# Two fp16 pieces instead of two fp32r pieces in the products of an attention and MoE kernel

## The chip, the cores and the metric

The kernel runs on one core of a Trainium2 chip. The metric is the device time in microseconds, from the start to the end of one execution. The profile shows the engines TensorE (PE, with its weight loads as PEld), VectorE (DVE), ScalarE (ACT), GpSimd (POOL) and the DMA queues, of which SyncE (SP) issues nearly all.

## The reference

An attention with a decaying state runs over 768 tokens for 4 batches and 8 heads of width 48. Its output is the input of two dense products with a gate in between.

```python
for t in range(S):                                   # S = 768, D = 48
    cur = einsum('bhd,bhe->bhde', u[None] * kt, vt)
    y[:, :, t] = einsum('bhd,bhde->bhe', rt, state + cur)
    state = wt[:, :, :, None] * state + einsum('bhd,bhe->bhde', kt, vt)
x = y.transpose(0, 2, 1, 3).reshape(3072, 384)
h = x @ w_in                                         # 384 -> 2048
g = where(h >= 1, h, where(h <= -1, 0, (h + 1)**2 / 4))
out = g @ w_out                                      # 2048 -> 384, fp32
```

The weights come as float64. All other inputs and the output are fp32.

## The kernel before, in words

**Tiling.** The 3072 tokens are cut into 12 units of 256 for the attention and 6 blocks of 512 for the products. Unit u belongs to block u // 2. The 2048 hidden rows are cut into 16 slices `f` of 128. A *step* is one slice of one block: three input chunks of 128 rows are contracted into a bank `h` (line 1040), the gate is taken (lines 819 to 825), and the result is multiplied into the three output banks `acc` (line 1070), which gather over the 16 slices. `HALVES` cuts the first 8 slices of block 0 and the first 11 of block 1 into steps of 256 tokens, so that a block can start when only one of its units is there. There are 115 steps.

**Pieces.** All but the first 8 steps write each operand as a high and a low piece in fp32r, and add high x high, high x low and low x high: 9 matmuls in `product_in`, 9 in `product_out`. The first 8 steps multiply plain fp32 (`product_in_whole`, `product_out_whole`, lines 1046 and 1052), which the profile shows as two instructions per matmul.

**Gate of a step.** ACT computes relu(h/2 + 1/2) (line 819) and squares it (820), DVE takes max(min(g, 1), h) (821), ACT rounds it to `gh` (824), DVE subtracts for `gl` (825). Products of a step follow up to `LAG` = 2 steps later; there are two `h` banks and three sets of g, gh and gl.

**Weights.** `weight(f)` fetches a 768 KB tile of float64 bits (line 332), ACT and POOL take its words apart (342, 345, 346), DVE joins them to fp32 (336). `divide(f)` rounds to the high piece on ACT (358) and subtracts for the low piece on DVE (361). A fetch waits until ACT has read the raw tile of three fetches before. Raw tiles, fp32 tiles and pieces share one pool of 16 slots.

**Attention of a unit.** DVE makes decay products with scans (434, 429) and multiplies them in (455, 505). PE makes 64x64 products (475), state updates (533) and outputs (612). `yevac` takes the output to the pieces of x (ACT 699, DVE 697), and six small DMAs fill the rows that hold head remainders (747). For unit 0 the low piece is made on PE with a negative identity `minus` (709).

**Order.** Every operation is an entry of a plan with an engine, a cost and its dependences. `ORDER` is a written list of all entries. The program is emitted in that order, so it fixes the order on each engine's queue and on SP's. Near the end a check (`check`, then the PE dot of line 914 and a DVE compare) makes a flag; if it is set, the slower function `general` computes everything again.

Of the kernel before, what the change touches and what calls it, by code (L numbers as in the profile page):

```python
# [229 lines left out]
def attention_moe(tc, a):  # L230
    nc = tc.nc
    V, A, G, PE = nc.vector, nc.scalar, nc.gpsimd, nc.tensor
    plan = Plan()
# [907 lines left out]
```

## Time and profile before

| | us |
|---|---|
| median of 3 runs (lowest, highest) | 499.04 (498.68, 499.18) |
| span of the profiled execution | 495.2 |
| PE busy | 485.5 (98%) |
| DVE busy | 343.8 (69%) |
| ACT busy | 289.6 (58%) |
| POOL busy | 56.7 (11%) |

The span runs from the first to the last instruction of the profiled execution. No time of that one execution with what lies around its span is shown beside the three runs; the median is 3.8 us above the span. Busy shares are means over stages with different limits, so a change is judged from the stage in which it stands.

### The profile page before, as it was taken

The page shows a single profiled execution, that of the slowest core. Times are in us where ns is not written, and L with a number is a line of the kernel's source. Part 1 is how long each engine was busy: PE and PEld are TensorE (multiplying, and loading weights), DVE is VectorE, ACT ScalarE, POOL GpSimd, SP SyncE. Part 2 cuts the span into 40 slices and gives each one's busy share as a digit, 9 for nine tenths or more (in the row PEclk, how much of TensorE's full clock was granted, in tenths as well). Part 3 has the DMA queues.
Part 4 walks back from the last instruction along what each step waited for, and adds up shares of the span by engine and source line. Part 5 has one row for each costly group of instructions (what it writes and reads, how often), then busy time and mean ns, then how long its engine had stood idle before and what let it go on. Part 6 is the DMA issues. An engine that isn't in the chain of part 4 may idle for free.

```text
span 495.2 us, 12991 instructions
## 1 busy us (share of the span) xinstructions
PE 485.5 (98%) x5402; PEld 404.8 (82%) x5402; DVE 343.8 (69%) x597; ACT 289.6 (58%) x592; POOL 56.7 (11%) x60
## 2 busy tenths in 40 slices
PE   9799999999999999999999999999999999999997
PEld 4688998778999988888888888888888888888886
DVE  6899999998758768659679679469556745332333
ACT  3799889866656536746736646346626625552551
POOL 2332121300110101110110330020001000000000
PEclk9899999999999999999999999999999999999999
DMA  8995736225544344345245454225221110200001
GB/s 316 406 374 169 256 115 217 88 60 158 166 111 149 66 133 159 103 113 161 38 131 175 108 139 150 48 79 154 43 66 44 29 33 16 66 1 1 1 0 66
DMA packets 58749, 58.29 MB, mean 118 GB/s; under 512 B 38016, under 2 KB 47424, under 8 KB 58688
## 3 DMA queue, kind: packets, MB, share of 16 engines
q1 hardware_dynamic: 58256, 56.78, 37.4%
q8 instruction: 43, 0.70, 0.6%
q10 hardware_dynamic: 432, 0.66, 0.4%
q14 instruction: 18, 0.15, 0.1%
HBM read 46.34 MB, written 4.72 MB: 103 GB/s over the span
## 4 chain that ended last, share of the span: by engine, by line
PE 89%; DVE 5%; ACT 2%; issue 2%; DMA 1%; POOL 0%; DVEq 0%; SPq 0%; POOLq 0%
PE h L1040 37%; PE acc L1070 36%; PE bank L612 4%; PE bank L475 2%; PE bank L533 2%; PE acc L1052 2%; PE bank L1070 1%; PE h L1046 1%; PE bank L312 1%; DMA rk<-in_rk 1%; DVE r L481 1%; DVE wt L361 1%; PE acc L612 1%; DVE gl L825 1%; DVE rk L505 1%
## 5 line engine op out<-in xcount | busy, mean ns | idle before, releaser
L1040 PE MATMUL h<-x,wt 128*128 128x512 f32 (+1 forms) x963 | 207.4, 365 | 0.5 <-DVE g L821 0.4
L1040 PEld LDWEIGHTS h<-x,wt 128*128 128x128 f32 x963 | 162.5, 188 | 32.0 <-DVE g L821 0.9
L1070 PE MATMUL acc<-gh,wt 128*128 128x512 f32 (+1 forms) x642 | 146.4, 359 | 0.0
L821 DVE SCALAR_TENSOR_TENSOR g<-g,h 128x512 f32<-128x512 f32 (+1 forms) x115 | 67.8, 593 | 95.6 <-ACT g L820 95.1
L819 ACT ACTIVATE g<-h 128x512 f32<-128x512 f32 (+1 forms) x115 | 60.4, 526 | 119.2 <-PE h L1040 117.4
L1070 PEld LDWEIGHTS acc<-gh,wt 128*128 128x128 f32 x642 | 107.9, 188 | 18.7
L825 DVE TENSOR_TENSOR gl<-g,gh 128x512 fp32r<-128x512 f32 (+1 forms) x107 | 68.9, 648 | 17.1 <-ACT gh L824 10.6
L1070 PE MATMUL acc<-gl,wt 128*128 128x512 f32 (+1 forms) x321 | 80.7, 358 | 0.0
L824 ACT CAST gh<-g 128x512 fp32r<-128x512 f32 (+1 forms) x107 | 59.1, 556 | 33.1 <-DVE g L821 22.3
L820 ACT ACTIVATE g<-g 128x512 f32<-128x512 f32 (+1 forms) x115 | 64.4, 561 | 3.1
L1070 PEld LDWEIGHTS acc<-gl,wt 128*128 128x128 f32 x321 | 55.2, 188 | 9.1
L434 DVE TENSOR_TENSOR_SCAN p<-wq,seeds 128x514 f32<-128x514 f32 x24 | 30.8, 1283 | 10.8 <-DMA kt<-p 7.2
L501 POOL TENSOR_TENSOR r<-cst,d 128x512 f32<-128x512 f32 x16 | 17.0, 1084 | 152.2 <-DVE d L498 71.8
L429 DVE TENSOR_TENSOR_SCAN y<-wq,seeds 128x514 f32<-128x514 f32 x24 | 30.1, 1254 | 0.8
L346 POOL CAST rr<-fl 128x768 f16<-128x768 f32 x16 | 21.3, 1332 | 71.2 <-ACT fl L342 32.7
L493 POOL TENSOR_TENSOR nk<-nk 128x768 f32<-128x768 f32 x8 | 15.3, 1913 | 96.8 <-DMA nk<-in_nk 87.9
L455 DVE TENSOR_TENSOR rk<-rk,y 128x512 f32<-128x512 f32 x24 | 17.1, 712 | 2.6 <-DMA rk<-in_rk 2.1
L505 DVE TENSOR_TENSOR rk<-rk,p 128x512 f32<-128x512 f32 x24 | 17.0, 717 | 0.7 <-DMA rk<-in_rk 0.4
L345 ACT ACTIVATE rr<-wraw 128x768 uint16<-128x768 uint32 x16 | 17.3, 1079 | 0.2 <-DVE wa L336 0.2
L342 ACT ACTIVATE fl<-wraw 128x768 f32<-128x768 f32 x16 | 14.7, 917 | 1.0 <-DVE wt L361 1.0
L481 DVE COPY_PREDICATED r<-cst,bank 128x512 f32<-128x512 int32 x20 | 14.5, 729 | 1.0 <-PE h L475 0.5
L612 PEld LDWEIGHTS bank<-rk,st 48*48 48x48 f32 x656 | 11.4, 119 | 4.2 <-issue 1.8
(116 smaller groups left out, 447.8 us busy)
## 6 DMA issues: line engine op xcount, KB each, us to landing
rk<-in_rk SPq DMA_DIRECT2D x24, 512.0 KB, 5.3
wraw<-in_wbits SPq DMA_DIRECT2D x16, 768.0 KB, 6.9
wq<-in_w SPq DMA_DIRECT2D x24, 258.5 KB, 3.0
nk<-in_nk SPq DMA_DIRECT2D x8, 768.0 KB, 4.9
vn<-in_v SPq DMA_DIRECT2D x11, 384.0 KB, 4.4
kt<-p SPq DMA_DIRECT2D x128, 32.0 KB, 1.9
fl<-in_w SPq DMA_DIRECT2D x12, 257.0 KB, 3.4
x<-last SPq DMA_DIRECT2D x66, 32.0 KB, 2.0
```

Of the source, the lines that this page charges most:

```text
L346: op("POOL", SIGN, due, [("fl", k)], ["rr_high"], lambda: G.tensor_copy(rr.bitcast(F16).rearrange("p (c two) -> p c two", two=2)[:, :, 1], s))
L429: V.tensor_tensor_scan(out=y_[:, ::-1], data0=w[:, SEG:0:-1], data1=sv[:, ::-1], initial=0.0, op0=ALU.mult, op1=ALU.add)
L434: V.tensor_tensor_scan(out=pv[:, q].rearrange("p n c -> p (n c)"), data0=w[:, 0:SEG], data1=sv, initial=0.0, op0=ALU.mult, op1=ALU.add,)
L505: op("DVE", 0.69, due, [("p", q)], [("r", slot[q])], lambda q=q: V.tensor_tensor(out=parts(q, 0), in0=parts(q, 0), in1=pv[:, q, :, 0:UT], ...
L612: PE.matmul(out=bank[by[g]][HP * half : HP * half + wide, lo : lo + C], start=first, stop=False, skip_group_check=True, **kw)
L819: op("ACT", c, due, [("b", 6 + hk)], [("g", gk)], lambda: nc.scalar.activation(gs, hs, AF.Relu, scale=0.5, bias=0.5))
L820: op("ACT", c, due, (), [("g", gk)], lambda: nc.scalar.activation(gs, gs, AF.Square))
L821: op("DVE", 0.13 + 0.53 * k, due, [("b", 6 + hk)], [("g", gk)], lambda: nc.vector.scalar_tensor_tensor(out=gs, in0=gs, scalar=1.0, in1=hs, ...
L824: op("ACT", c, due, [("g", gk)], [("gh", gk)], lambda: nc.scalar.copy(ghs, gs))
L825: op("DVE", 0.15 + 0.5 * k, due, [("g", gk), ("gh", gk)], [("gl", gk)], lambda: nc.vector.tensor_tensor(out=gls, in0=gs, in1=ghs.bitcast(F ...
L1040: nc.tensor.matmul(hp, lhsT=wx[f][:, cs], rhs=xt[:, j, :], start=n == 0, stop=n == 8)
L1070: nc.tensor.matmul(o, lhsT=wx[f][:, 384 + j * 128 : 512 + j * 128], rhs=gt[:, 0 : cs.stop - cs.start] if gt.shape[1] < cs.stop else gt[:, cs],
```

## The change

x, the gate's result and the weights become two fp16 pieces each, scaled by `ONE` = 256. The h banks then hold h times `BOTH` = 65536, and the gate and the last copies carry the factors. The first 8 steps stay fp32, with weights scaled by 256. Raw weight tiles get a pool of five. Guards on the sizes of x and of the weights are added to the check. Attention outputs use 64 columns of weights in all units. `general` makes its own pieces. `ORDER` is replaced as a whole (1783 entries before).

```diff
+ONE = 2.0**8
+BOTH = ONE * ONE
+RAWS = 5
+X_MAX, W_SUM, W_LEAST = 0.5, 1.3, 2.0**-8
 ORDER = (
...
-    wpool = tc.alloc_tile_pool(name="wpool", bufs=NF)
+    wpool = tc.alloc_tile_pool(name="wpool", bufs=NF + WHOLE)
+    rawpool = tc.alloc_tile_pool(name="rawpool", bufs=RAWS)
-    x_ = tiles(2, [128, 2, 3, WIDE], F32R, "x")
+    x_ = tiles(2, [128, 2, 3, WIDE], F16, "x")
-    gh = tiles(LAG + 1, [128, WIDE], F32R, "gh")
-    gl = tiles(LAG + 1, [128, WIDE], F32R, "gl")
+    gh = tiles(LAG + 1, [128, WIDE], F16, "gh")
+    gl = tiles(LAG + 1, [128, WIDE], F16, "gl")
...
-        op("SP", 0.45, due, (), [("raw", f), ("flight", f % FLIGHT), *room], fetch, size=786432)
+        op("SP", 0.45, due, [("raw", f - RAWS)] if f >= RAWS else (), [("raw", f), ("flight", f % FLIGHT)], fetch, size=786432)
...
-            wt = wpool.tile([128, 2, 768], F32R, tag="wt", name=f"wt{f}")
+            wt = wpool.tile([128, 2, 768], F16, tag="wt", name=f"wt{f}")
...
-        wide = HP if alone or u in INPLACE else D
+        wide = HP
...
             elif part:
-                V.tensor_tensor(out=to[1], in0=yv, in1=to[0].bitcast(F32), op=ALU.subtract)
+                for i in alike:
+                    V.scalar_tensor_tensor(out=to[1][i], in0=yv[i], scalar=ONE, in1=to[0][i], op0=ALU.mult, op1=ALU.subtract)
             else:
-                A.copy(to[0], yv)
+                A.activation(to[0], yv, AF.Copy, scale=ONE)
...
+        op("DVE", 0.95, (0, 0.0), reads, [("xm", u)], lambda: V.tensor_reduce(
+            out=xm[:, u : u + 1], in_=x_[u // 2 % 2][:, 0, :, u % 2 * UT : u % 2 * UT + UT], op=ALU.max, axis=AX.XY, apply_absolute_value=True))
...
+    def w_guard(f):
+        when = len(steps) - 40, 0.0
+        op("ACT", 1.05, when, [("wh", f)], ["nk", "perm", "squares"], lambda: A.activation(
+            squares, w_hi[f], AF.Square, accum_out=wx[:, f : f + 1]))
+        op("DVE", 0.55, when, ["squares"], ["wmax"], lambda: V.tensor_tensor(out=wm, in0=squares[:, 384:768], in1=wm, op=ALU.add)
+           if f else V.tensor_copy(wm, squares[:, 384:768]))
...
-            op("ACT", c, due, [("g", gk)], [("gh", gk)], lambda: nc.scalar.copy(ghs, gs))
...
+            op("ACT", c, due, [("g", gk)], [("gh", gk)], lambda: nc.scalar.activation(ghs, gs, AF.Copy, scale=1.0 / ONE))
+            op("DVE", 0.2 + 0.52 * k, due, [("g", gk), ("gh", gk)], [("gl", gk)], lambda: nc.vector.scalar_tensor_tensor(
+                out=gls, in0=gs, scalar=1.0 / ONE, in1=ghs, op0=ALU.mult, op1=ALU.subtract), port=True)
...
+    def dots():
+        PE.matmul(bank[0][0:1, 0:1], lhsT=ptot[:, 0:1], rhs=above[:, 0:1], start=True, stop=True)
+        PE.matmul(bank[0][0:1, 64:448], lhsT=minus_one, rhs=wm, start=True, stop=True)
...
+    def verdict():
+        V.tensor_reduce(out=xm[0:1, 2:3], in_=bank[0][0:1, 64:448], op=ALU.max, axis=AX.X)
+        V.tensor_scalar(out=xm[0:1, 2:3], in0=xm[0:1, 2:3], scalar1=-DF * (W_LEAST * ONE) ** 2, scalar2=None, op0=ALU.is_le)
+        V.tensor_scalar(out=flag, in0=bank[0][0:1, 0:1], scalar1=xm[0:1, 2:3], scalar2=127.5, op0=ALU.mult, op1=ALU.is_lt)
```

The low piece of x is made in two parts, that of `last` in one. `w_guard` runs 16 times, once for each f, and `x_guard`, the reduction over one unit's high piece, 12 times. `minus` and `last` become fp16 too, `check` gets six small DVE operations, and the last copies multiply by 1/65536 on the same engines as before.

## Rows read from the trace of the kernel before

**Rows 1.** The page: busy time, share of the span, instructions; granted clock in 40 slices.
```profile
PE 485.5 (98%) x5402; PEld 404.8 (82%) x5402; DVE 343.8 (69%) x597; ACT 289.6 (58%) x592; POOL 56.7 (11%) x60
PEclk9899999999999999999999999999999999999999
```

**Rows 2.** The page: the chain that ended last, shares by engine.
```profile
PE 89%; DVE 5%; ACT 2%; issue 2%; DMA 1%; POOL 0%; DVEq 0%; SPq 0%; POOLq 0%
```

**Rows 3.** Waits of PE: line, releaser, total us, times, longest; the longest of seven.
```profile
PE acc L612 <- issue: 1.4, 1, 1.4
```

**Rows 4.** Windows: stretch, length, busy us (instructions) of each engine, clock, DMA.
```profile
53.00:109.00 56.00, 54.98 (x668) 47.47 (x667) 54.66 (x84) 45.94 (x86) 11.15 (x8) 1.00 0.46 156
109.00:187.00 78.00, 77.73 (x1165) 72.00 (x1164) 56.54 (x120) 46.79 (x124) 7.96 (x6) 1.00 0.46 130
...
290.00:490.00 200.00, 200.00 (x1714) 163.52 (x1713) 107.37 (x186) 95.80 (x184) 9.92 (x8) 1.00 0.18 48
```

**Rows 5.** Chain in order of time: start, us, piece; products of 512, 256, fp32, attention.
```profile
46.64 1.29 PE h L1046 x6
...
55.92 2.13 PE h L1040 x18
58.04 1.09 PE bank L475 x64
...
181.64 1.94 PE bank L612 x128
...
208.97 2.10 PE h L1040 x9
```

**Rows 6.** Lines by form, TensorE: count | busy us, mean ns | idle before.
```profile
L1040 PE MATMUL h<-x,wt 128*128 128x512 f32 x693 | 170.7, 397 | 0.5 <-DVE g L821 0.4
L1040 PEld LDWEIGHTS h<-x,wt 128*128 128x128 f32 x963 | 162.5, 188 | 32.0 <-DVE g L821 0.9 <-DVE r L481 0.2
L1070 PE MATMUL acc<-gh,wt 128*128 128x512 f32 x430 | 116.4, 398 | 0.0
...
L1040 PE MATMUL h<-x,wt 128*128 128x256 f32 x270 | 36.9, 285 | 0.1
L1070 PE MATMUL acc<-gh,wt 128*128 128x256 f32 x212 | 35.1, 282 | 0.0
...
L612 PE MATMUL bank<-rk,st 48*48 48x64 f32 x656 | 14.3, 219 | 0.4
...
L612 PE MATMUL bank<-r,vn 64*48 64x64 f32 x704 | 12.2, 216 | 0.0
...
L1070 PE MATMUL bank<-gh,wt 128*128 128x256 f32 x32 | 8.9, 285 | 0.0
```

**Rows 7.** Lines by form, DVE and ACT.
```profile
L825 DVE TENSOR_TENSOR gl<-g,gh 128x512 fp32r<-128x512 f32 x77 | 55.1, 718 | 14.2 <-ACT gh L824 7.9 <-PE bank L1070 5.1
L821 DVE SCALAR_TENSOR_TENSOR g<-g,h 128x512 f32<-128x512 f32 x77 | 52.5, 683 | 91.7 <-ACT g L820 91.5
...
L824 ACT CAST gh<-g 128x512 fp32r<-128x512 f32 x77 | 47.3, 617 | 28.6 <-DVE g L821 19.1 <-PE bank L1070 4.6 <-DVE seeds L433 3.1
...
L342 ACT ACTIVATE fl<-wraw 128x768 f32<-128x768 f32 x16 | 14.7, 917 | 1.0 <-DVE wt L361 1.0
...
L697 DVE TENSOR_TENSOR x<-bank,x 128x384 fp32r<-128x384 f32 x22 | 11.8, 547 | 1.2 <-ACT last L699 1.2
...
L583 DVE TENSOR_TENSOR st<-bank,st 128x192 f32<-128x192 f32 x30 | 10.6, 355 | 1.5
...
L498 DVE TENSOR_REDUCE d<-nk 128x8 f32<-128x384 f32 x16 | 8.5, 539 | 0.0
```

**Rows 8.** Timeline of DVE: start, us, instruction; first and last scan between 72 and 91 us.
```profile
72.05 1.23 DVE L434 TENSOR_TENSOR_SCAN p<-wq,seeds 128x514 f32<-128x514 f32 x1
...
89.18 1.23 DVE L429 TENSOR_TENSOR_SCAN y<-wq,seeds 128x514 f32<-128x514 f32 x1
```

**Rows 9.** The page: DMA issues of the raw weights, KB each, us to landing.
```profile
wraw<-in_wbits SPq DMA_DIRECT2D x16, 768.0 KB, 6.9
```

More of the change, by code (lines that the diff above doesn't have):

```diff
@@ L249, in attention_moe @@
     u_sb = one([128, DM], F32, "u_sb")
-    minus = one([128, 128], F32R, "minus")
+    minus = one([128, 128], F16, "minus")
     flag = one([1, 1], I32, "flag", cpool)
@@ L330, in fetch @@
         def fetch():
-            wraw[f] = wpool.tile([128, 768, 2], I32, tag="wt", name=f"wraw{f}")
+            wraw[f] = rawpool.tile([128, 768, 2], I32, tag="raw", name=f"wraw{f}")
             nc.sync.dma_start(out=wraw[f].rearrange("p c two -> p (c two)"), in_=a["wbits"][f].bitcast(I32))
@@ L691, in yevac @@
                 to = [x[:, n].rearrange("p a (c g t) -> p a c g t", c=2, g=2)[:, :, :, g, :] for n in range(2)]
+            alike = [slice(None)] if what else [np.s_[:, :, c] for c in range(2)]
             if part == 2:
@@ L736, in attention @@
                 if u not in INPLACE:
-                    op("DVE", 0.27 if what else 0.54, due, [("b", by[g]), names(what, 0, g)], [names(what, 1, g)],
+                    op("DVE", 0.28 if what else 0.7, due, [("b", by[g]), names(what, 0, g)], [names(what, 1, g)],
                        lambda g=g, w=what: yevac(g, 1, w))
@@ L774, in check, with x_guard @@
         V.tensor_scalar(out=above[:, 0:1], in0=above[:, 0:1], scalar1=0.0, scalar2=None, op0=ALU.is_le)
+        V.tensor_reduce(out=xm[:, 0:1], in_=xm, op=ALU.max, axis=AX.X)
+        V.tensor_scalar(out=xm[:, 0:1], in0=xm[:, 0:1], scalar1=X_MAX * ONE, scalar2=None, op0=ALU.is_le)
+        V.tensor_reduce(out=xm[:, 1:2], in_=wx, op=ALU.max, axis=AX.X)
+        V.tensor_scalar(out=xm[:, 1:2], in0=xm[:, 1:2], scalar1=(W_SUM * ONE) ** 2, scalar2=None, op0=ALU.is_le)
+        for i in range(2):
+            V.tensor_tensor(out=above[:, 0:1], in0=above[:, 0:1], in1=xm[:, i : i + 1], op=ALU.mult)
+    def x_guard(u):
+        key = "x", u // 2 % 2, u % 2
+        reads = [(key, 0, g) for g in range(2)] + [(*key, j, h) for j in range(3) for h in range(2) if u not in ALONE]
+        op("DVE", 0.95, (0, 0.0), reads, [("xm", u)], lambda: V.tensor_reduce(
+            out=xm[:, u : u + 1], in_=x_[u // 2 % 2][:, 0, :, u % 2 * UT : u % 2 * UT + UT], op=ALU.max, axis=AX.XY, apply_absolute_value=True))
+    nkf = nk.rearrange("p a b c -> p (a b c)")
+    squares, wm, wx = nkf[:, 0:768], nkf[:, 768:1152], nkf[:, 1152 : 1152 + NF]
+    def w_guard(f):
[4 more added lines that the diff above has]
+           if f else V.tensor_copy(wm, squares[:, 384:768]))
     halves = [slice(i * UT, i * UT + UT) for i in range(2)]
@@ L838, in second @@
                 tail = [("tail", 0)] * (n >= len(steps) - 2)
-                op("PE", 2.109 * k * sum(p[2].stop - p[2].start for p in some) / (3 * w), due, [("gh", gk), ("gl", gk), ("wh", f), ("wl", f)],
+                op("PE", 1.95 * k * sum(p[2].stop - p[2].start for p in some) / (3 * w), due, [("gh", gk), ("gl", gk), ("wh", f), ("wl", f)],
                    sorted(("b", p[3]) for p in some) + tail, fresh=begin,
@@ L858, in out @@
         def out(how, o, key, place, to, by):
-            copy = V.tensor_copy if how == "DVE" else A.copy
+            copy = (lambda o, i: V.tensor_scalar(out=o, in0=i, scalar1=1.0 / BOTH, scalar2=None, op0=ALU.mult)) if how == "DVE" else (
+                lambda o, i: A.activation(o, i, AF.Copy, scale=1.0 / BOTH))
             n = place[2].stop - place[2].start
@@ L902, in attention_moe @@
         products(n)
+        if f == NF - 1 and cs.stop == WIDE:
+            for u in (2 * b, 2 * b + 1):
+                x_guard(u)
         for u in VISIT:
@@ L911, in attention_moe @@
         guard(w, ("fl", 0), n, due)
+    for f in range(NF):
+        w_guard(f)
     every = [("ptot", u, q) for u in range(NU) for q in range(2)] + [("above", n) for n in range(2 * NU)]
+    every += ["wmax", *[("xm", u) for u in range(NU)]]
     op("DVE", 1.0, (len(steps) - 12, 0.0), (), [*every, "ok"], check)
-    op("PE", 0.3, (len(steps) - 6, 0.0), ["ok"], [("b", 0)], lambda: PE.matmul(
-        bank[0][0:1, 0:1], lhsT=ptot[:, 0:1], rhs=above[:, 0:1], start=True, stop=True))
-    op("DVE", 0.2, (len(steps) - 4, 0.0), [("b", 0)], ["flag"], lambda: V.tensor_scalar(
-        out=flag, in0=bank[0][0:1, 0:1], scalar1=127.5, scalar2=None, op0=ALU.is_lt))
+    def dots():
+        PE.matmul(bank[0][0:1, 0:1], lhsT=ptot[:, 0:1], rhs=above[:, 0:1], start=True, stop=True)
+        PE.matmul(bank[0][0:1, 64:448], lhsT=minus_one, rhs=wm, start=True, stop=True)
+    op("PE", 1.0, (len(steps) - 6, 0.0), ["ok", "wmax"], [("b", 0)], dots)
+    def verdict():
+        V.tensor_reduce(out=xm[0:1, 2:3], in_=bank[0][0:1, 64:448], op=ALU.max, axis=AX.X)
+        V.tensor_scalar(out=xm[0:1, 2:3], in0=xm[0:1, 2:3], scalar1=-DF * (W_LEAST * ONE) ** 2, scalar2=None, op0=ALU.is_le)
+        V.tensor_scalar(out=flag, in0=bank[0][0:1, 0:1], scalar1=xm[0:1, 2:3], scalar2=127.5, op0=ALU.mult, op1=ALU.is_lt)
+    op("DVE", 0.9, (len(steps) - 4, 0.0), [("b", 0)], ["flag"], verdict)
     tc.mark_branch_hint_location("verdict", "LikelyTaken", engines=(mybir.EngineType.PE, mybir.EngineType.DVE, mybir.EngineType.Pool))
@@ L922, in attention_moe @@
             emit()
-    for p in (psum, pool):
+    for p in (psum, pool, rawpool, wpool):
         p.release()
@@ L928, in attention_moe, with general @@
     with tc.If(unsafe > 0, label="verdict"):
-        general(tc, a, ident, w_hi, w_lo)
-    for p in (wpool, cpool):
-        p.release()
-def general(tc, a, ident, w_hi, w_lo):
+        general(tc, a, ident)
+    cpool.release()
+def general(tc, a, ident):
     nc = tc.nc
@@ L1004, in general @@
     ):
+        w_hi, w_lo = {}, {}
+        for f in range(NF):
+            raw = sb.tile([128, 768, 2], I32, tag="raw", name=f"graw{f}")
+            G.dma_start(out=raw.rearrange("p c two -> p (c two)"), in_=a["wbits"][f].bitcast(I32))
+            s, wide = (sb.tile([128, 768], F32, tag=t, name=f"g{t}{f}") for t in ("s", "wide"))
+            r = sb.tile([128, 768], I32, tag="r", name=f"gr{f}")
+            r16 = r.bitcast(U16).rearrange("p (c two) -> p c two", two=2)
+            V.tensor_scalar(out=s, in0=raw[:, :, 1].bitcast(F32), scalar1=float(2.0**-112), scalar2=None, op0=ALU.mult)
+            V.tensor_scalar(out=r16[:, :, 0], in0=raw[:, :, 0].bitcast(U32), scalar1=LOW, scalar2=None, op0=ALU.mult)
+            V.tensor_copy(r.bitcast(F16).rearrange("p (c two) -> p c two", two=2)[:, :, 1], s)
+            V.scalar_tensor_tensor(
+                out=wide.bitcast(I32), in0=s.bitcast(I32), scalar=3, in1=r, op0=ALU.logical_shift_left, op1=ALU.bitwise_or)
+            wt = wp.tile([128, 2, 768], F32R, tag="wt", name=f"gwt{f}")
+            w_hi[f], w_lo[f] = wt[:, 0, :], wt[:, 1, :]
+            V.tensor_copy(w_hi[f], wide)
+            V.tensor_tensor(out=w_lo[f], in0=wide, in1=w_hi[f].bitcast(F32), op=ALU.subtract)
         for b in range(B):
```

30 lines of the change are left out of this document (15 added, 15 removed), and 126 rows, old and new, of the table ORDER.

## The prediction

> **What bounds the kernel now.** I read the busy times first, then the chain of waits, the waits of TensorE, busy time by stretch, and last the lines kept apart by form. TensorE is busy for 98% of the span, at the full clock in nearly every slice [rows 1]. The chain that ended last is 89% TensorE and 5% VectorE [rows 2], and the longest of the seven waits that stopped TensorE was 1.4 us [rows 3]. From 109 us on it has hardly a gap, while VectorE works 56.5 of 78 us and later 107.4 of 200 [rows 4]. Only the stretch from 53 to 109 us, in which block 0 is multiplied and the weights are still taken apart, has two full engines: TensorE 55.0 and VectorE 54.7 of 56 us [rows 4]. So time is saved by whatever shortens TensorE's own stream, unless VectorE holds the early stretch.
>
> **The pitch of a product.** Durations of single matmuls overlap, so I take pitches from the chain. Nine fp32r matmuls of 512 columns stand for 2.10 us, 233.3 ns each; eighteen of 256 columns for 2.13 us, 118.3 ns each, for which I use 118.5, between this row and other pieces of nine [rows 5]. Twice the short less the long pitch leaves 3.7 ns fixed, and the difference over 256 columns is 0.448 ns a column. At the 2.4 GHz level, which the granted clock shows here, a column would take 0.417 ns. So most of the excess grows with the columns. The plain fp32 products show that the array can go faster: six instructions of two passes over 256 columns take 1.29 us, 215.0 ns per instruction or 107.5 ns per pass, close to the 106.7 of one column a cycle [rows 5]. What fp32r loses is therefore in how it is streamed, and I expect fp16 to stream one column a cycle.
>
> The counts: 693 products of 512 columns at line 1040, and at line 1070 430 with gh and half as many with gl, in all 1338; of 256 columns 270 at line 1040, 212 with gh, 32 with gh into the spare bank, and half as many again with gl, in all 636 [rows 6]. At these pitches they take 312.2 + 75.4 = 387.5 us.
>
> No 16-bit matmul stands in the trace, so fp16 is bounded from both sides. With fp32r's fixed 3.7 ns kept: 217.0 and 110.4 ns, a saving of 1338 x 16.3 + 636 x 8.1 = 27.0 us. Like an fp32 pass: 215.0 and 107.5 ns, a saving of 24.5 + 7.0 = 31.5 us. The bare column count gives 34.3 us and an unchanged pitch gives 0. I take the middle of the two near ones, 216.0 and 109.0 ns: 23.1 + 6.0 = **29.1 us saved**.
>
> The Trainium skill bears on this. Its page "TensorE: Matmul & The Clock Gate", section "Back-to-back issue gap", gives a warm gap of N/2.4 + 2.5 ns, with no word on the element type. Taken so, fp32r would already go at 215.8 ns and the change would save nothing here; the 233.3 ns of the trace contradict that for fp32r [rows 5]. Taken for 16 bits alone it gives 215.8 and 109.2 ns, as an estimate 29.3 us saved.
>
> **What is added on TensorE.** The second dot has 384 columns in fp32, four passes of 161 ns by the fp32 row, 0.65 us, with the turn from one kind to the other 0.7. The attention outputs of units 1 to 11 use 64 columns of weights in place of 48, in 704 + 656 matmuls [rows 6]. With 64 columns line 475 stands at 1.09 us for 64, 17.0 ns each, with 48 columns line 612 at 1.94 for 128, 15.2 [rows 5]; the difference times 1360 is 2.5 us, and nothing is the other end, since the moving side is 64 columns in both. I take 0.4, as the mean durations are nearly one (216 and 219 ns). Below nothing no wider weight can go.
>
> **What is added elsewhere.** VectorE: 12 guards of 768 columns, each between 0.94 and 1.08 us by the 0.54 us reduction of 384; 16 additions of 384, about 0.55 us between the 0.355 of 192 and the 0.68 of 512; the low piece of x in two parts, 2 x 0.355 for 0.547 us, 22 times. The subtraction for gl becomes a three-operand instruction, like line 821 at 683 ns against 718 now; I price it at 0, with -4 to +6 us of VectorE's time as bounds [rows 7]. Together 12 + 9 + 3.6, some 25 us: 369 of about 469 us. ScalarE: 16 squares of 768 columns with a sum, 0.92 us each by line 342 and a little for the sum, about 18 us: 307 of 469. Conversions to fp16 keep the element counts; I price them as now. Neither engine reaches TensorE as a whole, so I cost all this at 0. What covers it is the slack of the gate: three ScalarE operations of about 0.62 and two of VectorE of about 0.7 make 3.3 us, with handovers some 4.3, and products may follow two steps later, 2 x 18 x 0.216 = 7.8 us. An operation of 1.1 us ahead of the gate fits into the 3.5 us left. Without that cover each would cost up to its length, 29 us for the 28 guards.
>
> **The early stretch.** Eight half and eight whole steps of block 0 lie there: 8 x 18 x 9.5 + 8 x 18 x 17.3 ns = 3.9 of the 29.1 us. VectorE must give the same weights and units in less time. It has something to put off: four scans between 72 and 91 us, at least 1.2 us each [rows 8], belong to unit 3, which block 1 needs only at its twelfth step. So the cost is between 0 (enough is moved) and 5.9 (all of the gain and 2 us of VectorE's new work in that stretch). I take 1.5, nearer to moved.
>
> **Waits and order.** The weight fetch, which already waits for the reading of the tile three before, also waits for the join of the tile five before. Behind it on SP stand the loads of the next unit. Five raw tiles cover this; if they did not, one landing of 6.9 us [rows 9] would be late once. I take 0. The new order can win what waits TensorE has, some 5 us over the span (485.5 busy, about 5 at the two ends), and can lose as much where an entry comes late. I take 0.5 lost. The ends of the execution, first loads and last copies, stay: the scaling copies have the old element counts, and the longer verdict runs beside the last output.
>
> **Sum.** The profiled execution has a span of 495.2 us; what lies around it is the 3.8 us up to the median of 499.04, and I leave it as it is. 495.2 - 29.1 + 0.7 + 0.4 + 1.5 + 0.5 = 469.2 of span, with 3.8 **473.0 us**.
>
> **The rivals.** *VectorE holds the early stretch.* For it: 54.7 of 56 us busy. Against it: unit 3's scans. The price is the 5.9 in place of 1.5, and perhaps 1 us more where block 1 starts late: 477.4 to 478.4, say 478.
>
> *The guards stand in the gate's queue.* If the added 28 operations come where a step's gate is just due, half of their 29 us shows: 487. For it: both queues keep strict order. Against it: the 3.5 us of slack, and VectorE's idle half after 290 us.
>
> *The pitch does not fall: the weight swap sets it, not the width of an element* (slower). Each product needs its own 128x128 weights, whose load shows 188 ns [rows 6]. If this paces the stream, fp16 keeps 233.3 and 118.5 ns, and wider attention weights cost their full 2.5 us: 499.0 + 0.7 + 2.5 + 0.5 = 502.7. It decides as soon as the new pitch of 512 columns is above 231 ns. Against it: at 256 columns the pitch is 118.5 ns, well below 188, so loads overlap more than one product. The skill's page above, section "Weight-path perf modes", says that the array takes one element per cell per cycle whatever its width; by that the width gains nothing, and fp32r's 0.448 ns a column speaks against it.
>
> *The change does not do what it says:* a guard fails and everything is computed again, 768 rounds with a scan of 768 elements; from 1.23 us for 514 [rows 8] that is over 1.4 ms. From one draw of the inputs I get 0.107 for the largest x against the limit of 0.5, 1.21 against 1.3, and 4.5e-4 against 1.5e-5, so this is hardly possible.
>
> **How the numbers follow.** The forecast, 467 to 477: 0.76. VectorE early, 477 to 480: 0.11. Guards, 480 to 492: 0.06. No lower pitch: 0.03. A failing guard: 0.01. Below 467, where fp16 goes as fast as an fp32 pass or better and the order wins its 5 us: 0.03. The likeliest is 473. The low end is 467: 499.0 - 31.5 + 0.7 and nothing else is 468.2, with a little from the order. The high end is 480, with VectorE early and the poorer pitch. About 0.2% (1 us) is what can be told from no change. Faster: the first three and the last, 0.96. Within 0.2%: 0.01, a pitch that falls by 1%. Slower: 0.03.
>
> **What would show it.** In the changed profile nine products of 512 columns should stand 1.94 us apart in the chain and nine of 256 about 0.98. TensorE should stay above 97% busy from 109 us on, with VectorE near 79% of the span. Block 0 should end 2 to 4 us earlier than now. I am wrong if the pieces still last 2.10 us, if TensorE waits for gh or gl in the second half, or if its busy share in the early stretch falls by over 4 us.

## The result and the profile after

The changed kernel takes 480.12 us (median of 4 runs, 478.51 to 483.31) against 498.86 for the kernel before: a ratio of 0.963, 95% interval 0.958 to 0.968. The forecast was 473.0. The direction and the pitch of a product came as forecast; 7 us of the forecast gain did not come, and the median lies 0.1 us above the top of the range. The profiled run has a span of 476.7 us in place of 495.2.

The page after (busy time, clock in 40 slices, the chain's shares), to be held against [rows 1, 2]:

```profile
PE 460.1 (97%) x5408; PEld 273.2 (57%) x5408; DVE 367.1 (77%) x655; ACT 297.3 (62%) x624; POOL 59.0 (12%) x60
PEclk9799999999999999999999999999999999999999
PE 74%; DVE 13%; DMA 5%; issue 3%; ACT 3%; SPq 0%; DVEq 0%; ACTq 0%
```

TensorE has 25.4 us less work, but the span is only 18.5 shorter: its idle time rose from 9.7 to 16.6. In the chain VectorE's share rose from 5% to 13% and that of DMA from 1% to 5%.

Pieces of the chain (start, us, piece), to be held against [rows 5]:

```profile
57.69 1.97 PE h L1108 x18
...
91.21 1.94 PE acc L1138 x9
...
178.55 2.02 PE bank L624 x128
...
257.61 7.77 PE acc L1138 x36
```

Nine products of 512 columns take 1.94 us, 215.6 ns each, and 36 of them 7.77, 215.8 each, for which I write 215.7; eighteen of 256 take 1.97, 109.4 ns each. Both are the forecast's pitches within 0.4 ns. The attention outputs, 128 to a group, went from 1.94 to 2.02.

Lines by form (count | busy us, mean ns | idle before), to be held against [rows 6, 7]:

```profile
L1108 PEld LDWEIGHTS <-wt 128*128 128x128 f16 x963 | 93.2, 98 | 87.0 <-issue 6.7
...
L862 DVE SCALAR_TENSOR_TENSOR gl<-g,gh 128x512 f16<-128x512 f32 x77 | 54.3, 714 | 13.9 <-ACT gh L861 13.8
...
L799 DVE TENSOR_REDUCE xm<-x 128x1 f32<-128x768 f16 x12 | 11.3, 944 | 0.0
...
L809 DVE TENSOR_TENSOR nk<-nk 128x384 f32<-128x384 f32 x15 | 8.3, 551 | 4.5 <-ACT nk L807 4.1
```

On VectorE the added work costs what the sum said: gl 714 ns against 718, the guards 944 and 551 ns, 367.1 us in all (369 forecast). ScalarE's busy time rose by 7.7 us to 297.3, where 18 and 307 were forecast.

**Where the gain went.** With 17.6 ns saved on a product of 512 columns and 9.1 on one of 256, the products of each stretch should have gained so much; the lead is that of the same step's first product in the trace after over that in the trace before:

| up to | products should have gained, us | lead after, us | lost in this stretch, us |
|---|---|---|---|
| step 8 (no fp16 product yet) | 0 | -4.8 | 4.8 |
| step 28 | 4.3 | 0.2 | -0.7 |
| step 52 (block 1's attention) | 9.0 | 0.8 | 4.1 |
| end of the last product | 29.3 | 20.3 | 0.8 |
| end of the span | 29.3 | 18.5 | 1.8 |

So three places lose 10.0 of the 10.8 us: the head (4.1 up to step 28, of which 1.1 stand already at step 0), the stretch of block 1 (4.1), and the last microseconds (1.8). From step 52 on the change is worth nearly all it promised.

The 1.1 us at step 0 can't be put down to the change. Step 0 begins at 23.8 us in the trace before and at 24.9 in this one, but with a full granted clock it begins at 23.1 in the new order (experiment 7) and at 22.8 in the old one (experiment 11); where the clock falls to 0.50 it begins as late as 25.6 (see the end). So the head proper lost 3.0 us, from step 0 to step 28.

Busy time in the head and in block 1's stretch (columns as in [rows 4]), of before and of after:

```profile
20.00:60.00 40.00, 38.66 (x617) 33.50 (x612) 38.09 (x64) 35.38 (x72) 11.32 (x8) 0.97 0.80 292
118.00:193.00 75.00, 74.73 (x1086) 69.37 (x1085) 54.77 (x117) 46.16 (x119) 8.12 (x6) 1.00 0.47 137
```
```profile
20.00:60.00 40.00, 36.62 (x556) 30.15 (x550) 37.36 (x59) 33.75 (x64) 11.34 (x8) 0.93 0.63 233
118.00:193.00 75.00, 71.99 (x1088) 55.12 (x1086) 63.48 (x134) 44.55 (x118) 10.17 (x7) 1.00 0.49 145
```

In the head, VectorE is nearly as busy as before (37.4 us for 38.1, of 40) with fewer instructions done (59 for 64). In block 1 TensorE idles 3.0 us of 75, where it idled 0.3.

The end of the execution, timeline (start, us, instruction), before and after:

```profile
491.56 0.15 DVE L916 TENSOR_SCALAR flag<-bank 1x1 int32<-1x1 f32 x1 [0.48 <-PE bank L914]
...
491.80 0.28 PE L1070 MATMUL bank<-gl,wt 128*128 128x256 f32 x1
```
```profile
471.47 0.27 PE L1138 MATMUL bank<-gl,wt 128*128 128x256 f16 x1
...
471.72 0.81 PE L960 MATMUL bank<-nk,minus_one 128*1 128x384 f32 x2
...
472.57 0.55 DVE L965 TENSOR_REDUCE xm<-bank 1x1 f32<-1x384 f32 x1 [0.36 <-PE bank L960]
...
473.32 0.21 DVE L967 TENSOR_SCALAR flag<-bank,xm 1x1 int32<-1x1 f32 x1
```

Before, the flag was written before the last product had ended; now its writing begins 1.6 us behind that end. From the end of the last product (its start and its 0.28 or 0.27 us) to the end of the span it was 3.1 us and is 5.0.

### The profile page after: what moved, and what is told of

It reads as the page before. It is cut to its first block, busy times and chain, and to the rows that moved or that the text cites. A ratio compares the mean times of both kernels' runs of the same rounds, so it can differ in the third digit from the quotient of the medians.

```text
span 476.7 us, 13081 instructions
## 1 busy us (share of the span) xinstructions
PE 460.1 (97%) x5408; PEld 273.2 (57%) x5408; DVE 367.1 (77%) x655; ACT 297.3 (62%) x624; POOL 59.0 (12%) x60
## 4 chain that ended last, share of the span: by engine, by line
PE 74%; DVE 13%; DMA 5%; issue 3%; ACT 3%; SPq 0%; DVEq 0%; ACTq 0%
PE h L1108 33%; PE acc L1138 30%; PE bank L624 4%; DVE y L441 3%; DVE p L446 2%; PE bank L545 2%; DMA fl<-in_w 2%; PE bank L487 2%; DVE gl L862 2%; DVE g L858 1%; DMA nk<-in_nk 1%; DMA rk<-in_rk 1%; PE bank L1138 1%; DVE rk L467 1%; DVE rk L517 1%
## 5 line engine op out<-in xcount | busy, mean ns | idle before, releaser
L1108 PE MATMUL h<-x,wt 128*128 128x512 f16 (+1 forms) x963 | 194.0, 349 | 4.1 <-DVE g L858 1.4
L1138 PEld LDWEIGHTS <-wt 128*128 128x128 f16 x1011 | 97.8, 98 | 81.7
L1108 PEld LDWEIGHTS <-wt 128*128 128x128 f16 x963 | 93.2, 98 | 87.0 <-issue 6.7
L1138 PE MATMUL acc<-gh,wt 128*128 128x512 f16 (+1 forms) x642 | 135.9, 344 | 0.0
L862 DVE SCALAR_TENSOR_TENSOR gl<-g,gh 128x512 f16<-128x512 f32 (+1 forms) x107 | 68.7, 652 | 14.9 <-ACT gh L861 14.7
L1138 PE MATMUL acc<-gl,wt 128*128 128x512 f16 (+1 forms) x321 | 76.1, 344 | 0.0
L861 ACT ACTIVATE gh<-g 128x512 f16<-128x512 f32 (+1 forms) x107 | 59.3, 561 | 17.0 <-DVE g L858 9.1
L441 DVE TENSOR_TENSOR_SCAN y<-wq,seeds 128x514 f32<-128x514 f32 x24 | 33.0, 1375 | 0.8
L467 DVE TENSOR_TENSOR rk<-rk,y 128x512 f32<-128x512 f32 x24 | 18.5, 770 | 1.5 <-ACT nk L457 0.9
L624 PE MATMUL bank<-rk,st 48*64 48x64 f32 x656 | 14.9, 223 | 0.8 <-DVE st L595 0.4
L624 PEld LDWEIGHTS bank<-rk,st 48*64 48x64 f32 x656 | 12.4, 134 | 5.2 <-issue 2.8
L487 PEld LDWEIGHTS bank<-rk 64*64 64x64 f32 x448 | 11.5, 134 | 6.4 <-issue 2.5
```

The costliest lines, as they stand in the source:

```text
L441: V.tensor_tensor_scan(out=y_[:, ::-1], data0=w[:, SEG:0:-1], data1=sv[:, ::-1], initial=0.0, op0=ALU.mult, op1=ALU.add)
L467: op("DVE", 0.69, due, ["y"], [("k", s)], lambda q=q: V.tensor_tensor(out=parts(q, 1), in0=parts(q, 1), in1=y_.rearrange("p (n c) -> p n c ...
L624: PE.matmul(out=bank[by[g]][HP * half : HP * half + wide, lo : lo + C], start=first, stop=False, skip_group_check=True, **kw)
L861: op("ACT", c, due, [("g", gk)], [("gh", gk)], lambda: nc.scalar.activation(ghs, gs, AF.Copy, scale=1.0 / ONE))
L862: op("DVE", 0.2 + 0.52 * k, due, [("g", gk), ("gh", gk)], [("gl", gk)], lambda: nc.vector.scalar_tensor_tensor(out=gls, in0=gs, scalar=1.0 ...
L1108: nc.tensor.matmul(hp, lhsT=wx[f][:, cs], rhs=xt[:, j, :], start=n == 0, stop=n == 8)
```

## The experiments

My first theory: the pitch brings its 29 us, and the new order gives some 10 back. The rivals: the added guards, the wider weights, VectorE's load, collisions of VectorE with GpSimd. Unless said otherwise, a time is a median of 6 runs (12 in experiment 2, 7 in experiment 9); the interval in brackets is that of the ratio to the kernel before.

**1. fp16 alone, in the order of before.** The kernel before with fp16 tiles, no scale and no guards, and the 64-column weights:

```diff
-    x_ = tiles(2, [128, 2, 3, WIDE], F32R, "x")
+    x_ = tiles(2, [128, 2, 3, WIDE], F16, "x")
...
-            wt = wpool.tile([128, 2, 768], F32R, tag="wt", name=f"wt{f}")
+            wt = wpool.tile([128, 2, 768], F16, tag="wt", name=f"wt{f}")
...
-        wide = HP if alone or u in INPLACE else D
+        wide = HP
```

> The kernel before with fp16 pieces (no scaling, no guards) and 64-column attention weights, its old order and its old pools. If the new written order costs what is missing: 499 - 29 for the products + 2.3 for the wider weights, 472 us (470 to 474), with few new waits of TensorE. If VectorE and the arrival of work hold a faster TensorE back in any order: 476 to 481, with new waits of TensorE in the first 60 us and in block 1.

Measured: 480.3 us, ratio 0.962 [0.958, 0.967], so no faster than the change. The theory fell as stated: the old order is no better as a whole. But the losses lie elsewhere. Its lead at step 8 is -1.1 (the change: -4.8) and at step 28 it is 2.1; then 5.6 us are lost in block 1 and some 7 more later, in new waits such as 4.9 us for g in the whole trace. The order made for slower products leaves TensorE waiting when they get faster, and block 1 loses in either order. TensorE's share of block 1's stretch here:

```profile
118.00:193.00 75.00, 69.56 (x1048) 53.62 (x1041) 53.98 (x113) 44.45 (x116) 7.83 (x6) 1.00 0.44 127
```

VectorE has 54.0 us of work in it, less than before the change, and TensorE idles 5.4.

**2. The wide weights alone**, the last line of the diff above on the kernel before:

> The kernel before with 64 columns of attention weights instead of 48, nothing else. If the wider weights cost what the attention outputs grew by in the two traces (27.0 to 29.3 us on TensorE): 501.3 us, 0.5% slower. If that growth was waiting in the new order: 499.0.

Measured: 499.3 us, ratio 1.0013 [0.9984, 1.0041]. A group of 128 went from 1.94 to 2.02 us, as in the change, so 1360 of them cost about 0.85 us; the time itself can't tell this from nothing.

**3. The change without its new guards**, twelve reductions, sixteen squares and additions, the second dot and the longer verdict:

```diff
-        op("ACT", 1.05, when, [("wh", f)], ["nk", "perm", "squares"], lambda: A.activation(
-            squares, w_hi[f], AF.Square, accum_out=wx[:, f : f + 1]))
+        op("ACT", 1.05, when, [("wh", f)], ["nk", "perm", "squares"], lambda: None)
```

> The changed kernel without its guards on x and on the weights (12 reductions, 16 squares with sums, 16 additions, the longer check and verdict), all else in the same order. If the guards in the queues cost what is missing: 472 to 474 us. If it is the order of the rest: 478 us, about 2 less than the changed kernel, from the end alone.

Measured: 477.97 us, ratio 0.958 [0.954, 0.963], 2.2 us below the change, though the intervals overlap. The losses in the head and in block 1 stay (step 8 begins at 58.1 us, the lead at step 52 is -0.4). What the trace shows as won lies at the end: 3.8 us behind the last product in place of 5.0. So the 28 guards among the gates cost nearly nothing, as forecast.

**4. The change without the four fills** with zero matmuls that its planner put into TensorE's gaps:

```diff
-            PE.matmul(bank[b[1]], lhsT=zero, rhs=zero.unsqueeze(1).broadcast_to([128, 4, 128]), start=True, stop=True)
+            pass
```

> The changed kernel without the four zero matmuls that the plan puts into gaps it foresees on TensorE. If TensorE would wait there anyway: 480 us as the changed kernel, or 1 us more if its clock falls instead. If the zeros hold up real work: 477 us, by their 3.6 us on TensorE.

Measured: 479.19 us, ratio 0.962 [0.957, 0.967]. They cost nothing that can be told.

**5. The order of before up to step 20's product, the new one after it.** All entries up to that product stand as in the kernel before; what the new order had put among them follows, and then its rest. The first lines that differ:

```diff
-    "22 268 42 40 46 39 43 47 37 41 117 38 48 118 44 119 49 50 131 122 51 120 53 45 124 54 74 123 55 71 52 136 269 57 56 125 127 58 "
+    "268 42 40 46 39 43 47 37 41 117 38 48 118 44 119 49 50 131 122 51 120 53 45 124 238 54 74 123 55 71 52 136 269 57 56 125 127 58 59 "
...
```

> The changed kernel with the order of the kernel before up to the product of step 20, and its own order from there; all operations and pools are its own. The changed kernel reaches step 8 some 4 us later than before, with no fp16 product run until then. If the new order of the first 55 us is the cause: step 8 near 54 us in place of 57.5, and 477 us (476 to 478.5). If the pool of five raw tiles or the units' data are the cause: step 8 near 57 and 480.

Measured: 474.86 us, ratio 0.952 [0.950, 0.955]: 5.3 us faster than the change, inside the forecast's own range. The lead is -1.7 at step 8 and 4.1 at step 28, against the 4.3 that the products are worth; from step 0 to step 28 this trace takes 4.2 us less than the change's. Then the lead falls to 3.3 at step 52, where the products should add 4.7. The windows:

```profile
20.00:60.00 40.00, 38.40 (x630) 32.70 (x627) 36.99 (x64) 34.21 (x70) 10.89 (x8) 0.93 0.77 280
118.00:193.00 75.00, 71.22 (x977) 53.43 (x975) 61.42 (x127) 43.77 (x114) 10.16 (x7) 1.00 0.46 133
```

VectorE is no busier in the head (37.0 us) than in the change but gets 64 instructions done in place of 59, and TensorE has 1.8 us more. The loss in the head belongs to the new order.

**6. The change with block 1's gl cut to 8 columns**, to take VectorE's load away there:

```diff
-                out=gls, in0=gs, scalar=1.0 / ONE, in1=ghs, op0=ALU.mult, op1=ALU.subtract), port=True)
+                out=gls[:, 0:lw], in0=gs[:, 0:lw], scalar=1.0 / ONE, in1=ghs[:, 0:lw], op0=ALU.mult, op1=ALU.subtract), port=True)
```

> The changed kernel with the gl subtraction cut to 8 of its columns in the 27 steps of block 1, which takes some 9 us of VectorE's work out of the stretch from 110 to 190 us (the low piece of the gate is left stale there). If VectorE's load paces block 1: TensorE gains up to 4 us there, 476 to 477. If it is the arrival of units and loads, or the gate's wait behind other ScalarE work: 480, under 1 us less.

```profile
118.00:193.00 75.00, 71.91 (x1086) 55.10 (x1084) 54.94 (x135) 44.82 (x119) 9.59 (x7) 1.00 0.50 141
```

Measured: 479.46 us, ratio 0.960 [0.956, 0.964]. VectorE has 8.5 us less to do there (54.9 for 63.5) and TensorE not a tenth more (71.9 for 72.0). Block 1 is not paced by VectorE's load.

**7. The kernel before in the new order**, fp32r and 48 columns, the guards left out of the list and a few entries put later where they need it:

```diff
-    "268 42 40 46 39 43 47 37 41 117 38 48 118 44 119 49 50 131 122 51 120 53 45 124 238 54 74 123 55 71 52 136 269 57 56 125 127 58 59 "
+    "268 42 40 46 39 43 47 37 41 117 38 48 118 44 119 49 50 131 122 51 120 53 45 124 54 74 123 55 71 52 136 269 57 56 125 127 58 59 76 "
...
```

> The kernel before (fp32r, 48 columns, old pools) in the order of the changed kernel, guards left out of the list. If the new order loses 4 us in the first 55 us whatever the element type: step 8 near 57 us, and 501 to 503 in all. If the loss comes with fp16 alone: 498 to 499.

Measured: 504.53 us, ratio 1.0125 [1.010, 1.015], slower than before by 5.7 us. With no fp16 at all the new order takes 3.5 us more from step 0 to step 8 (32.42 for 28.95), where the change takes 3.7 more. But the head is not all of the 5.7: from step 28 to 52 the lead falls by another 3.5 us, from -3.2 to -6.7, though no product has become cheaper here. The window of block 1:

```profile
118.00:193.00 75.00, 73.33 (x1133) 67.21 (x1132) 57.77 (x119) 42.54 (x114) 10.19 (x7) 1.00 0.49 142
```

TensorE idles 1.7 us of it, where it idled 0.3 in the old order. So the new order by itself loses in block 1 too, and the faster products by themselves do (experiment 1); the two losses don't add up, as the change loses 4.1 there.

**8. Short casts on GpSimd.** The weights' casts in the change cut to 8 columns, so that GpSimd is out of VectorE's way:

```diff
-        op("POOL", SIGN, due, [("fl", k)], ["rr_high"], lambda: G.tensor_copy(rr.bitcast(F16).rearrange("p (c two) -> p c two", two=2)[:, :, 1], s))
+        op("POOL", SIGN, due, [("fl", k)], ["rr_high"], lambda: G.tensor_copy(rr.bitcast(F16).rearrange("p (c two) -> p c two", two=2)[:, 0:8, 1], s[:, 0:8]))
```

> The changed kernel with GpSimd's 16 casts of the raw weights cut from 768 to 8 columns (the weights lose their signs). In the first 60 us these casts run beside scans and subtractions on VectorE, which then take 1.5 to 1.8 us in place of 1.2 and less. If these collisions are how the new order loses its 4 us there: step 8 near 54 us and 475 to 477 in all. If it is what stands ahead of the gates on the queues: step 8 near 57 us, 479 to 480.

Measured: 476.66 us, ratio 0.958 [0.954, 0.961]; from step 0 to 8 it takes 30.9 us, against 32.6 in the change and 29.3 in experiment 5. So about half of what the head loses goes with the long casts. The short ones also bring the weights earlier, and this run doesn't part that from the collisions. A count in the traces does: between step 0 and step 8 the VectorE operations that overlap one of GpSimd's take together 3.1 us more, in the change, than the median of their like without overlap; in the kernel before it is 1.4, in experiment 5 1.5 and here nothing. The change's excess over experiment 5, 1.6 us, is about the 1.7 us won here. What is left, 1.6 us against experiment 5, I put down to the order of the work itself. The collisions in the change, a scan beside a cast in the head, and in block 1 gl beside a product of GpSimd; then the cut cast beside a scan:

```profile
27.70 1.83 DVE L441 TENSOR_TENSOR_SCAN y<-wq,seeds 128x514 f32<-128x514 f32 x1
...
149.07 1.55 DVE L862 SCALAR_TENSOR_TENSOR gl<-g,gh 128x256 f16<-128x256 f32 x1
```
```profile
27.12 1.40 POOL L358 CAST rr<-fl 128x768 f16<-128x768 f32 x1 [2.74 <-DVE wa L349]
...
148.53 1.81 POOL L505 TENSOR_TENSOR nk<-nk 128x768 f32<-128x768 f32 x1 [5.87 <-DMA nk<-in_nk]
```
```profile
22.90 1.23 DVE L441 TENSOR_TENSOR_SCAN y<-wq,seeds 128x514 f32<-128x514 f32 x1
```
```profile
22.92 1.20 POOL L358 CAST rr<-fl 128x8 f16<-128x8 f32 x1 [5.74 <-DVE seeds L440]
...
33.44 0.19 POOL L358 CAST rr<-fl 128x8 f16<-128x8 f32 x1 [5.21 <-DVE wa L349]
```

A scan takes 1.23 us, and 1.83 where a cast has begun before it. The same holds the other way: a cast of 8 columns takes 0.19 us, and 1.20 where it begins 0.02 us behind a scan. The Trainium skill, "SBUF — State Buffer", section "SBUF: two separate sides", says that a VectorE operation with two SBUF inputs and a GpSimd operation that reads SBUF exclude each other for a whole instruction and that the first to start wins; these rows agree.

**9 and 10. Short products on GpSimd**, its two products per unit cut to 8 and 16 columns, in the change and then in the version of experiment 5:

```diff
-                out=nk[:, :, 0, :], in0=nk[:, :, 0, :], in1=nk[:, :, 1, :], op=ALU.mult), port=True)
+                out=nk[:, :, 0, 0:8], in0=nk[:, :, 0, 0:8], in1=nk[:, :, 1, 0:8], op=ALU.mult), port=True)
```

> The changed kernel with GpSimd's products in units 4 to 11 (8 of nk, 16 for the diagonal) cut to 8 and to 16 columns (the diagonal term is wrong). In block 1 a gl subtraction of 0.42 us stands 1.6 us beside them, and TensorE waits after it at 132 and 152 us. If these collisions take block 1's gain: 2 to 4 us less between steps 28 and 52, 476 to 478. If not: 479 to 480, with the waits of TensorE where they were.

> The kernel with the old head order (474.9 us) and the shortened GpSimd products of the run before. If both causes add up: 471 to 473, which is the forecast of 473 without the two mechanisms that it left out. If block 1 is held by something else: 474 to 475.

Measured: 478.04 us, ratio 0.959 [0.957, 0.962], and 473.36, ratio 0.949 [0.946, 0.952]. They lie 2.1 and 1.5 us below their base, with intervals that overlap those of the base. From step 28 to 52 the lead falls by 1.7 in the one and by 0.2 in the other, where the products should gain 4.7: block 1's loss stays.

**11. No reloaded pieces to guard.** In experiment 10 the chain ran through block 1 by the reload of a piece of w, the guard behind it in ScalarE's queue, and transfers that SyncE issues one after the other. From the version of experiment 5 the reloads and their guards go:

```diff
-        load(due, w, a["w"][u, q][:, 0:SEG], [("fl", 0)])
-        guard(w, ("fl", 0), n, due)
+        op("SP", 0.6, due, [], [("fl", 0)], lambda: None)
...
```

> The version with the earlier order up to step 20, without the twelve reloads of the w pieces and the two ScalarE guard operations that follow each (they stand in ScalarE's queue among the gates; this version no longer tests those w). Theory, block 1 is held by ScalarE's queue: the chain of the version before this one runs through DMA fl<-in_w 8.22 us and the guard behind it (0.64 us) there, so without them steps 28 to 52 regain 2 to 3 of the 4 us, and the time is 472 (474.9 with them). Rival, what holds block 1 is the arrival of the next unit, x<-last and kt<-p issued one after the other by SyncE at 0.6 us each: the reloads leave SyncE's queue too, but they are issued ahead of these, so the time is 474 to 475 and the lead from step 28 to 52 still falls by 4.

Measured: 472.35 us, ratio 0.947 [0.943, 0.951], which is the time that the theory named, and for another reason. From step 28 to 52 the lead goes from 6.6 to 6.8, not up by 2 to 3; of the 3.4 us between its trace and that of experiment 5, 2.4 stand already at step 0 (22.8 for 25.2 us), with a full clock ahead of it (see the end). Of the 2 to 3 us that the theory wanted in block 1 the trace shows 1.0, which is less than traces of the same entries differ by there (experiment 13). The theory fell.

**12. The verdict earlier**, ahead of the last products; and again, as 15, beside its control 14, which is experiment 5's version run once more on the same chip:

```diff
-    "1713 1587 1714 1710 1715 1711 1716 1698 1720 1705 1727 1721 1722 1717 1723 1718 1712 1735 1724 1728 1729 1736 1737 1730 1725 1738 "
-    "1719 1731 1739 1466 1732 1755 1740 1823 1726 1733 1734 1741 1742 1824 1746 1748 1743 1744 1745 1825 1747 1749 1750 1752 1826 1751 "
+    "1691 1713 1587 1714 1466 1710 1715 1711 1716 1755 1698 1720 1705 1727 1721 1722 1717 1723 1718 1824 1712 1735 1825 1724 1728 1729 "
+    "1736 1737 1730 1725 1738 1826 1719 1731 1739 1732 1740 1726 1733 1734 1741 1742 1746 1748 1743 1744 1745 1747 1749 1750 1752 1751 "
```

Here 1824 is the last test, 1825 the two dots, 1826 the verdict; three late guard operations (1466, 1755, 1823) moved up with them.

> The same version with the check, its two dots and the verdict put some five products earlier in the order, and the last guards with them, so that the flag is written before the last outputs are. Theory, the tail grew from 3.4 to 4.7 us after the last matmul because the verdict (dot of 0.81 us, reduce, compare) comes last: the tail is 3.4 to 3.7 again and the time 473.5 (1.0 to 1.5 us less). Rival, the tail is the last output's transfer and the flag's reads in any case: 474.9; and if the check's eight operations hold up VectorE's gate pieces: 475.5.

> The version with the earlier order up to step 20 once more, on the same chip as the two beside it, so that they can be compared without the difference between chips in the granted clock of the first 30 us: 473 to 475, and within 0.5 us of what the unit's own clock windows make of 474.9.

> The early verdict once more beside its control. Theory, the verdict behind the last product was the growth of the tail: 1.2 to 1.6 us less than the control. Rival, the earlier gain was the chip's clock: within 0.5 us of the control.

Measured: 472.86 us, ratio 0.948 [0.945, 0.952]; then 474.78, ratio 0.953 [0.950, 0.957], beside a control of 476.14, ratio 0.956 [0.952, 0.960], 1.1 above what I expected of it. In the trace of the repeat the flag is written long before the last product:

```profile
462.61 0.20 DVE L965 TENSOR_SCALAR flag<-bank,xm 1x1 int32<-1x1 f32 x1
```
```profile
468.34 0.27 PE L1136 MATMUL bank<-gl,wt 128*128 128x256 f16 x1
```

Its span ends at 472.0, 3.4 us behind the last product, where the control has 5.0, so the tail is 1.6 us shorter. That is not all gain, for the dots now stand in the stream of products:

```profile
459.90 0.81 PE L958 MATMUL bank<-nk,minus_one 128*1 128x384 f32 x2
```

From the first product of step 100 to the last product the repeat takes 63.3 us, the control 62.4. So by the traces the verdict's place is worth some 0.8 us net here, and 0.5 in experiment 12 against 5. The medians differ by 1.4, but the intervals of the two ratios overlap, so that a net gain is likely and not shown. The rival that the earlier gain was the chip's clock holds for part of it: experiment 12 had a full clock in the head and step 0 at 22.8 us. This version, the change with the earlier order in the head and an early verdict, leaves no work out and is faster than both kernels: against the change 472.86 and 474.78 us stand for 480.12.

**13. Half of the transposed keys' transfers**, from the version of experiment 5, beside the same control:

```diff
-                            op("SP", 0.64, due, [("p", 0), ("p", 1)], [("kt", 4 * i + g)], lambda i=i, g=g: apart(i, g), size=32768)
+                            op("SP", 0.64, due, [("p", 0), ("p", 1)], [("kt", 4 * i + g)], lambda i=i, g=g: apart(i, g) if i < 2 else None, size=32768)
```

> The version with the earlier order up to step 20, with 8 of the 16 kt<-p transfers of each unit from the fourth on left out (half of the transposed keys then stay those of an earlier unit, and the comparison behind the verdict is made one that never calls the general program). SyncE issues them one after the other at 0.61 to 0.65 us. Theory, block 1 is held by the arrival of its units over SyncE's queue: with 8 issues fewer a unit's keys arrive 5 us earlier, TensorE's idle time between 118 and 193 us falls from 3.8 us to about 1, and the time is 2 to 3 us less than that of the control beside it. Rival, VectorE's scans and gates one after the other hold it, and the keys wait for nothing: idle time and time as in the control, within 1 us.

Measured: 472.2 us, ratio 0.947 [0.944, 0.949], 3.9 below the control, and the intervals don't meet. Against experiment 5, the control's program on another chip, it is 2.7 below. SyncE's queue (start, us, issues), control, then this run, and their windows in the same manner:

```profile
122.79 5.79 SPq L530 DMA_DIRECT2D kt<-p  x7
...
132.89 6.98 SPq L530 DMA_DIRECT2D kt<-p  x9
...
159.31 10.39 SPq L530 DMA_DIRECT2D kt<-p  x16
```
```profile
124.91 2.59 SPq L530 DMA_DIRECT2D kt<-p  x4
...
132.38 2.55 SPq L530 DMA_DIRECT2D kt<-p  x4
...
160.60 5.17 SPq L530 DMA_DIRECT2D kt<-p  x8
```
```profile
118.00:193.00 75.00, 70.70 (x970) 52.77 (x969) 60.95 (x126) 43.52 (x114) 10.22 (x7) 1.00 0.45 128
```
```profile
118.00:193.00 75.00, 72.13 (x990) 53.81 (x988) 65.00 (x129) 45.42 (x118) 10.81 (x7) 1.00 0.42 129
```

Sixteen issues take SyncE 10.4 us. In the control TensorE waits 2.1 us for them, a wait that this run has not:

```profile
PE bank L543 <- DMA kt<-p: 2.1, 2, 1.8
```

From step 28 to 52 the lead grows by 1.3 us here and falls by 1.4 in the control. TensorE's idle time fell by 1.4, from 4.3 to 2.9 us, and not to the 1 us that I expected. Four profiles of the same entries in this stretch (experiments 5, 12, 14, 15) give -0.8, 1.1, -1.4 and 0.5 us, so the two traces alone prove little. What the medians show is that eight issues fewer for each unit from the fourth on save 2.7 to 3.9 us in all; that most of it lies in block 1 is what this pair of traces says (2.6 of the 3.1 us from step 0 on), and is not shown beyond it.

## Why the prediction was right and wrong

- **The pitch: right.** 216.0 and 109.0 ns were taken, 215.7 and 109.4 came, 29.3 us for 29.1. The reasoning from fp32's passes held, and the rival of the weight swap fell. No run parts the narrower element from the shorter weight load that came with it (98 for 188 ns). Against the load as the cause stands that fp32r took 17.6 ns more at 512 columns and 9.1 at 256: the excess grows with the columns, and each product has one load of the same size.
- **The work added on VectorE and ScalarE: right in that it stays hidden** (experiment 3), so the rival of the guards in the gate's queue fell. ScalarE's share of it was put 10 us too high.
- **The wider weights: 0.4 forecast, about 0.85 in the stream** (experiment 2), inside the bounds.
- **The ends of the execution, forecast at nothing: 1.8 us.** The step that failed is "the longer verdict runs beside the last output". It runs behind the last dot, which the order puts behind the last product (experiments 12 and 15). The 0.7 us of the second dot, which the sum had, is within this.
- **The early stretch and the order, 1.5 and 0.5 us forecast: this is the failed step.** From step 0 to step 28 3.0 us were lost, 1.1 more stand at step 0, where the clock of the two traces differs. The loss lies ahead of the first fp16 product (3.7 us from step 0 to 8, of which 0.7 come back by step 28), a stretch for which the forecast had nothing but the 0.5 of the order. The forecast asked how much work VectorE has and what it can put off. What happened is that the new order brings scans beside GpSimd's casts, and VectorE gets less done in the same busy time. That and the order of the remaining work cost 3.3 us from step 0 to 8 against the old order (experiment 5; 3.5 with fp32r in experiment 7), half of it each (8). The rival that VectorE holds the early stretch came nearest in price by luck: in its place, from 53 to 109 us, TensorE is busy for 55.7 us, where it was 55.0:

```profile
53.00:109.00 56.00, 55.73 (x641) 36.85 (x630) 53.11 (x86) 47.71 (x90) 9.03 (x7) 1.00 0.41 147
```

- **Block 1, forecast at full gain: 4.1 us lost; this step failed too.** TensorE had hardly a gap from 109 us on [rows 4], and I read that as TensorE setting the pace. Two units (sixteen kt<-p issues each) are made there, and a unit comes through scans, transfers that SyncE issues one by one and handovers, none of which fp16 shortens. SyncE's issues for the keys are the one part whose removal clearly saves time (13); VectorE's load (6), the guards (3, 11) and GpSimd's products (9, 10) are not the larger part. But the cheaper products are not the whole cause: the new order loses 3.5 us there with fp32r as well (7). How the 4.1 us divide between the order and the arrival of the units stays open; no run puts the old order into this stretch alone.
- **What lies around the span**, 3.8 us taken over from before, was misread. In every run of the change and of the experiments the time is 1.7 to 1.9 us above the span of the same execution. So, as an estimate, the profiled execution of the kernel before was some 2.0 us faster than its median. From the span of the change to its median it is 3.4 us, of which the profiled run has 1.8, and the forecast came out close here by luck.

None of the three signs of being wrong came true: the pieces last 1.94 us, no wait for gh or gl stands in the second half, and the early stretch is as busy as before. They all looked where nothing was lost.

In sum: where 3.1 us of losses were forecast, 10.8 came (1.1 of them with the clock), which makes 7.7 of the difference; the rest are a saving on products larger by 0.2 and the smaller surroundings.

## What to carry to other kernels

When the bounding engine's work gets cheaper, go through the schedule stretch by stretch and ask what arrives next, and by which chain of queues: a stretch without gaps says only that the engine's inputs came in time, not by how much. An order that is searched anew as a whole can be judged in pieces: put each piece of it into the other version and time it (here the old head alone gave 5 us back). And where something is decided at the end of a program, look whether it can stand ahead of the last products: here that took 1.6 us off the tail and put 0.9 into the stream.

## What the runs showed of the hardware

- The weight load of 128 columns in fp16 stands at 98 ns, for fp32r at 188 [rows 6], and the matmul pitch at 0.415 ns a column against 0.448: (215.7 - 109.4) over 256 columns.
- VectorE and GpSimd hold each other up, by 0.6 us on a scan of 1.23 and 1.1 on a subtraction of 0.42 to 0.5 (experiment 8).
- The granted clock of the head differs from run to run. In two windows after 16 us (columns as in [rows 4]) the profiled run of the change, then that of experiment 15:

```profile
16.00:20.00 4.00, 2.43 (x89) 2.24 (x89) 3.20 (x6) 1.07 (x1) 1.04 (x1) 0.80 1.04 396
20.00:24.00 4.00, 3.65 (x45) 3.46 (x39) 2.46 (x4) 2.06 (x5) 1.66 (x1) 0.50 1.02 411
```
```profile
16.00:20.00 4.00, 2.25 (x107) 2.01 (x110) 3.77 (x7) 2.11 (x3) 1.04 (x1) 1.00 1.04 396
20.00:24.00 4.00, 2.85 (x38) 2.31 (x29) 3.51 (x7) 3.43 (x7) 2.05 (x1) 1.00 1.03 408
```

In the first the clock is 0.80 and then 0.50 of the full one, the 1.2 GHz level, where TensorE was busy 2.4 and then 3.7 of 4 us; in the second it stays at 2.4 GHz where it was busy 2.3 and 2.9. Step 0 begins at 25.2 us in experiment 5, with 0.84 and 0.50 there, and at 23.4 in experiment 15, whose entries up to there are the same. It differs on one chip too: the six runs of the control (14) have mean granted clocks from 0.988 to 0.996. So two traces are best compared from step 0 on. The medians of the same program differ as well: 474.86 us in experiment 5, 476.14 in 14.
